# Polysketch attention and an MLP on one core: key-value matrices and all rows of x through DRAM, weight 1 in one piece, a new hand-written order

## The chip, the core and the metric

The kernel runs on one core of a Trainium2 chip. A core has five engines that run at the same time and wait for each other by semaphores: TensorE (PE, matrix products), VectorE (DVE), ScalarE (ACT), GpSimd (POOL) and SyncE (SP, here only an issuer of transfers). Transfers between DRAM and the core's SBUF are issued by SP or ACT and carried out by 16 DMA engines. The metric is the device time of one execution in microseconds (us); less is better.

## The reference

Two blocks follow each other. The first is attention with a sketched polynomial kernel, with 4 batches, 4 heads, 1088 positions and 32 dimensions per head; the second is a layer norm and a two-layer MLP with a residual, on rows of 128 (the four heads side by side).

```python
def phi(x):                                   # r = 8 sketches each
    a = np.einsum('rd,bhsd->bhsr', S1, x)
    b = np.einsum('rd,bhsd->bhsr', S2, x)
    return np.einsum('bhsi,bhsj->bhsij', a, b).reshape(*x.shape[:-1], r * r)
q_p, k_p = (phi(q), phi(k))
kv = np.einsum('bhsf,bhsd->bhfd', k_p, v)     # 64 x 32 for each head
z = np.sum(k_p, axis=2)
num = np.einsum('bhsf,bhfd->bhsd', q_p, kv)
den = np.einsum('bhsf,bhf->bhs', q_p, z)[..., None] + 1e-06
x = (num / den)                               # -> (4, 1088, 128)
...
mu = np.mean(x, axis=-1, keepdims=True)
var = np.mean((x - mu) ** 2, axis=-1, keepdims=True)
xn = (x - mu) / np.sqrt(var + 1e-06) * g_ln
ch = np.maximum(xn @ w_ch1, 0.0) @ w_ch2      # 128 -> 512 -> 128
return (x + ch).astype(np.float32)
```

S1, S2, the two weights and g_ln come as 64-bit floating point where numpy made them so (S and the weights); the kernel has to decode their words itself. All products are in 32-bit floating point.

## The kernel before

Everything is one flat list of named operations, `PROGRAM`: each name calls a small function that issues a few instructions on one or more engines. An engine executes its own instructions strictly in the order of this list, and waits where an operand is not there yet. So the list sets, for each engine and for each issuer of transfers (SP, ACT), what stands in front of what. A letter after a name says which engine does it: S is SP, A is ACT, V is DVE, G is POOL. No planner works at run time.

**Opening.** `ld_w`, `ld_s`, `ld_g`, `ld`, `ld_v`, `ld_vr` load weights, S, g_ln, k and q, and v. `c_...` fill constants; `c_act` is ACT's first activation, which brings a table load with it. `fill n w` and `bump n` are matmuls on ones that nobody reads. The 64-bit words of S (0), weight 1 and weight 2 are decoded by `w_ex`, `w_bits`, `w_exf`, `w_mant`, `w_low`, `w_e2`, `w_e3`, `w_add`/`w_addlow` and `w_mul` on DVE, ACT and POOL; weight 1 in two halves of 256 columns, each with its own load. `s_heads`, `sk`, `sk_b`, `sk_8`, `sk_q` and `sk_2` set up the sketches. `c_cg` and `fold` (with `fold_cp`) put the mean and g_ln of the layer norm into weight 1.

**Attention, per batch b.** `turn_g`/`turn_r` transpose k on DVE; `k_feat` multiplies it with the sketches on PE, `k_tok` transposes the result back, `k_prod` forms the 64 products per position, `k_sum`, `k_zs`, `k_sc`, `k_sccp` work on z, and `k_val` sums products times v into the PSUM bank KV. `k_vcp` (ACT) copies this out four times over, `k_spr` (PE, two 128x128 transposes) turns it, `k_rcp` (ACT) copies the result to `kvr`. For q: `turn_h`/`turn_r`, `q_feat`, `q_tok`, `q_ac`, `q_den`, `q_rec`, `q_a2`, `q_prod` on PE, DVE and POOL give the 64 products per position, already divided by the denominator; `q_turn` transposes them on DVE. `num` then multiplies them with `kvr`: 32 products of 32x32 tiles, each of two matmul instructions, into four PSUM banks, and `num_cp`/`num_r` copy them to `xT`, which holds x transposed. The first half of batch 0 goes another way (`q_dir`, `q_ac0`, `q_b0`, `q_prod0`, `q_flip`, `f_spr`, `num0`), so that the MLP can start early.

**MLP, per chunk c.** Ten chunks: 0 to 7 are half a batch (4 tiles of 128 positions), 8 and 9 collect the left-over positions (1 tile). `hid` multiplies `xT` with one of four column blocks of weight 1 (PE), `relu` copies it out, `sec` (4 products of 128x128 per tile, PE) multiplies with weight 2, and `fin` (DVE), or `fin_a` and `fin_g` (ACT, POOL), scale by 1/std and add x. `store` and `store_r` write the result. For the residual and the statistics x is needed with positions on partitions. For chunks 1 to 7 it goes through DRAM: `row_turn` (DVE), `row_wr` (one write), `row_rd` (four reads per chunk). For chunks 0, 8 and 9 PE transposes it: `row_pe`, `row_cp`. `st_bn`, `st_ag` (DVE) and `st_pow` (POOL) form 1/std.

## Time and profile before

| what | value |
|---|---|
| median of 3 runs | 103.91 us (103.06 to 104.55) |
| profiled execution | 102.81 us, span 100.9 us, granted PE clock 0.998 |
| PE busy | 95.3 us, 94% of the span |
| DVE busy | 74.0 us, 73% |
| POOL busy | 58.4 us, 58% |
| ACT busy | 41.3 us, 41% |
| chain that ended last | PE 78%, DMA 5%, POOL 5%, DVE 2%, ACT 2% |
| moved by DMA | 13.85 MB in 12367 packets |

How to read the rows of the prediction: in a timeline or chain the first number is the start in us from the span's start, the second the duration in us; then engine, line of the kernel, operation, and `out<-in`; `x4` is a count of instructions put together. PEld is PE's weight load, which overlaps its matmuls. SPq and ACTq are transfers issued by SP or ACT. A bracket tells how long the engine sat idle before, and what ended that. In the 40 slices of the span each digit is a busy share in tenths.

### The profile page before, as it was taken

The page shows a single profiled execution, that of the slowest core. Times are in us where ns is not written, and L with a number is a line of the kernel's source. Part 1 is how long each engine was busy: PE and PEld are TensorE (multiplying, and loading weights), DVE is VectorE, ACT ScalarE, POOL GpSimd, SP SyncE. Part 2 cuts the span into 40 slices and gives each one's busy share as a digit, 9 for nine tenths or more (in the row PEclk, how much of TensorE's full clock was granted, in tenths as well). Part 3 has the DMA queues.
Part 4 walks back from the last instruction along what each step waited for, and adds up shares of the span by engine and source line. Part 5 has one row for each costly group of instructions (what it writes and reads, how often), then busy time and mean ns, then how long its engine had stood idle before and what let it go on. Part 6 is the DMA issues. An engine that isn't in the chain of part 4 may idle for free.

```text
span 100.9 us, 3433 instructions
## 1 busy us (share of the span) xinstructions
PE 95.3 (94%) x1355; PEld 68.7 (68%) x1355; DVE 74.0 (73%) x239; ACT 41.3 (41%) x119; POOL 58.4 (58%) x83
## 2 busy tenths in 40 slices
PE   5988999999999999999999999999999999999960
PEld 5765668656656779656588669854469758959950
DVE  2878989789999599699089549999559079661630
...
PEclk9999999999999999999999999999999999999999
...
GB/s 76 272 293 389 353 370 275 272 218 88 3 6 301 212 164 3 6 130 0 6 107 106 47 59 0 109 153 187 55 107 204 143 122 148 1 115 132 77 119 64
DMA packets 12367, 13.85 MB, mean 137 GB/s; under 512 B 2880, under 2 KB 8768, under 8 KB 12352
## 3 DMA queue, kind: packets, MB, share of 16 engines
...
## 4 chain that ended last, share of the span: by engine, by line
PE 78%; DMA 5%; POOL 5%; DVE 2%; ACT 2%; SPq 2%; issue 1%; ACTq 0%; POOLq 0%
PE bankO L859 8%; PE bankM L859 8%; DMA w_raw<-in_moe_w_ch_dram 5%; PE bankN L843 5%; PE bankK L560 5%; PE bankC L843 4%; PE bankK L843 4%; PE bankK L859 4%; PE bankB L843 3%; PE bankA L843 3%; PE bankD L843 3%; PE bankM L250 3%; PE bankA L859 3%; PE bankN L859 3%; POOL ob L888 2%; PE bankA L735 2%
## 5 line engine op out<-in xcount | busy, mean ns | idle before, releaser
L82 POOL TENSOR_TENSOR kp<-kf 128x1024 f32<-128x1024 f32 (+4 forms) x9 | 15.9, 1779 | 0.1
L827 POOL TENSOR_SCALAR va<-mv 128x4 f32<-128x4 f32 (+1 forms) x10 | 2.3, 228 | 18.2 <-DVE mv L822 17.7
L82 POOL TENSOR_TENSOR qp<-a,fq 128x1280 f32<-128x1280 f32 (+1 forms) x5 | 11.1, 2219 | 0.2
L859 PEld LDWEIGHTS bankO<-w,hT 128*128 128x128 f32 x80 | 9.7, 192 | 1.9 <-issue 1.9
L829 POOL TENSOR_TENSOR rstd<-va,mhalf 128x4 f32<-128x4 f32 (+1 forms) x10 | 10.3, 1034 | 0.8
L859 PE MATMUL bankO<-w,hT 128*128 128x128 f32 x80 | 10.4, 277 | 0.0
L859 PEld LDWEIGHTS bankM<-w,hT 128*128 128x128 f32 x72 | 9.0, 192 | 1.9 <-issue 1.9
L677 DVE STREAM_TRANSPOSE qpT<-qp 128x1280 f32<-128x1280 f32 (+1 forms) x7 | 9.6, 1365 | 0.0
L250 PE MATMUL bankM<-ones 128*128 128x256 f32 (+1 forms) x28 | 8.3, 440 | 1.2 <-DVE top L180 1.2
L859 PE MATMUL bankM<-w,hT 128*128 128x128 f32 x72 | 9.3, 275 | 0.0
L816 DVE BATCH_NORM_STATS2 st<-x 128x6 f32<-128x128 f32 x32 | 6.7, 272 | 2.5 <-issue 2.5
L250 PEld LDWEIGHTS bankM<-ones 128*128 128x128 f32 x28 | 5.7, 241 | 2.5 <-DVE top L180 1.2
L851 ACT ACTIVATE hT<-bankC 128x512 f32<-128x512 f32 (+1 forms) x6 | 3.3, 551 | 8.3 <-PE bankB L859 4.7
L843 PE MATMUL bankC<-xT,w 128*128 128x512 f32 x12 | 6.1, 592 | 0.0
L843 PE MATMUL bankN<-xT,w 128*128 128x512 f32 (+1 forms) x14 | 6.1, 516 | 0.0
L851 ACT ACTIVATE hT<-bankN 128x256 f32<-128x256 f32 (+1 forms) x6 | 3.0, 498 | 7.2 <-PE bankN L843 7.2
L82 POOL TENSOR_TENSOR a<-fq,rden 128x160 f32<-128x160 f32 (+1 forms) x6 | 2.8, 463 | 5.2 <-DVE rden L659 4.8
L560 PEld LDWEIGHTS bankK<-kp,vn 128*32 128x32 f32 x288 | 4.2, 110 | 2.3 <-issue 1.1
L851 ACT ACTIVATE hT<-bankK 128x512 f32<-128x512 f32 (+1 forms) x6 | 3.1, 522 | 6.2 <-PE bankK L843 5.3
L457 DVE STREAM_TRANSPOSE qT<-qn 128x512 f32<-128x512 f32 x8 | 5.5, 687 | 0.0
L843 PE MATMUL bankK<-xT,w 128*128 128x512 f32 (+1 forms) x12 | 5.4, 530 | 0.0
L735 PE MATMUL bankD<-qpT,kvr 32*32 32x288 f32 (+1 forms) x64 | 5.2, 386 | 0.0
...
## 6 DMA issues: line engine op xcount, KB each, us to landing
...
xd<-xh SPq DMA_DIRECT2D x5, 256.0 KB, 2.6
x<-xd SPq DMA_DIRECT2D x20, 64.0 KB, 2.0
out_dram<-ob SPq DMA_DIRECT2D x19, 64.0 KB, 1.7
out_dram<-ob ACTq DMA_DIRECT2D x13, 64.0 KB, 1.9
w_raw<-in_moe_w_ch_dram SPq DMA_DIRECT2D x2, 256.0 KB, 4.0
```

Source lines behind the costliest of these rows:

```text
L82: by[eng].tensor_tensor(out=o, in0=a, in1=b, op=ALU.mult)
L250: pe.matmul(M[0][:, 0:w], ones[:, 0:P], ones[:, 0:w], start=True, stop=True)
L457: dve.transpose(_ap(dst[b % 2], 0, P, P * 4 * half, [[32, 4], [P, 4], [1, 32]]), src[b][:, 512 * half : 512 * half + 512],)
L560: pe.matmul(KV[D * h : D * h + D, 0:F], vn[b][:, TW * h + D * u : TW * h + D * (u + 1)], kp[:, H * F * u + F * h : H * F * u + F * (h + 1) ...
L677: dve.transpose(_ap(qpT, 0, P, 32 * u0, [[32, u1 - u0], [TW, 8], [1, 32]]), qp[:, H * F * u0 : H * F * u1])
L735: pe.matmul(X[r][D * h : D * h + D, o : o + w], kvr[b % 2][rows, DM * f + D * h : DM * f + D * h + D], qpT[rows, c : c + w], start=(f == 0 ...
L816: dve.bn_stats(out=sts[slot(c)][:, 6 * t : 6 * t + 6], in_=row_ap(c, t))
L827: pool.tensor_scalar(out=vas[slot(c)][:, 0:n], in0=_ap(mvs[slot(c)], 0, P, 1, [[2, n]]), scalar1=1e-6, scalar2=None, op0=ALU.add)
L829: pool.tensor_tensor(out=rstds[slot(c)][:, 0:n], in0=vas[slot(c)][:, 0:n], in1=mhalf[:, 0:n], op=ALU.pow)
L843: pe.matmul(banks[z][:, 0:n], w1[:, P * j : P * (j + 1)], cols(c)[:, a : a + n], start=True, stop=True)
L851: act.activation(o, i, AF.Relu)
L859: pe.matmul(banks[z][:, DM * t : DM * (t + 1)], h[:, 512 * j + P * t : 512 * j + P * (t + 1)], w2[:, DM * j : DM * (j + 1)], start=(j == 0 ...
```

## The change

1. Weight 1 is loaded by one transfer (`ld_w S 1 0 4`, the first on SP) and decoded in one piece of 512 columns; `fold` and `fold_cp` also run in one piece. `ld_s A 1` now stands behind `c_act`.
2. `k_vcp`, `k_spr` and `k_rcp` are gone. Instead DVE transposes the KV bank in 32x32 blocks (`kv_turn`), one transfer writes it to DRAM (`kv_wr`), four transfers read it back into `kvr`, one for each group of 32 partitions (`kv_rd`).
3. `num` reads `kvr` in the new layout, and its inner loops change places: r (row group of the array) is now innermost, h (column group) outside it.
4. Chunks 0, 8 and 9 go through DRAM as well: `row_pe` and `row_cp` are not called any more.
5. Nearly all transfers are issued by SP: ACT keeps `ld_s A 1` and four stores at the end.
6. The order of the list is new throughout; three `fill 1 256` are added, `sk_0` is dropped, and some operations change engine (`sk_2` and `k_sccp 0` to DVE, `w_mant` of weight 2 to ACT, its `w_add` to DVE, and single `relu`, `num_cp`, `num_r`, `k_prod`, `q_ac`, `q_a2`, `q_prod` between engines).

```diff
-    kvc = const([P, 2 * P], F32, "kvc")
+    kvt = const([P, F], F32, "kvt", 2)
+    kvx = [dram.tile([P, F], F32, name=f"xdk{i}") for i in range(B)]
...
-    def k_vcp(eng, b):
-        copy(eng, _ap(kvc, 0, P, 0, [[P, 2], [32, 4], [1, 32]]),
-             _ap(KV, 0, P, 0, [[32, 2], [0, 4], [1, 32]]))
...
-    def k_spr(b):
-        for i in range(2):
-            pe.transpose(KV[:, 256 + P * i : 256 + P * (i + 1)], kvc[:, P * i : P * (i + 1)], ident)
...
-    def k_rcp(eng, b):
-        copy(eng, kvr[b % 2], KV[:, 256:512])
+    def kv_turn(b):
+        dve.transpose(kvt[b % 2], KV[:, 0:F])
...
+    def kv_wr(eng, b):
+        by[eng].dma_start(out=bass.AP(kvx[b].tensor, kvx[b].offset, [[F, P], [1, F]]), in_=kvt[b % 2])
...
+    def kv_rd(eng, b, r):
+        by[eng].dma_start(
+            out=_ap(kvr[b % 2], 32 * r, 32, 0, [[F, H], [1, F]]),
+            in_=bass.AP(kvx[b].tensor, kvx[b].offset, [[F, 32], [32 * F, H], [1, F]]),
+        )
...
     def num(b, u0, u1):
         w = 32 * (u1 - u0)
         for f in range(2):
-            for r in range(4):
-                for h in range(H):
+            for h in range(H):
+                for r in range(4):
...
-                        kvr[b % 2][rows, DM * f + D * h : DM * f + D * h + D],
+                        kvr[b % 2][rows, F * h + D * f : F * h + D * f + D],
...
-    through_dram = set((1, 2, 3, 4, 5, 6, 7, ))
+    through_dram = set((0, 1, 2, 3, 4, 5, 6, 7, 8, 9))
```

The new list, cut to the parts that the prediction follows (the opening up to `num 1`, and the stretch from `num 2` to `num 3`):

```diff
+    c_ones; ld_w S 1 0 4; c_small; c_kvb; ld_s S 0; fill 1 128; c_act; ld_s A 1; c_iota; c_vpad 3;
+    ld S k 0 16 34; c_pads 0; fill 4 256; c_rest; ld S k 0 0 16; c_vpad 2; c_ac 1; ld S q 0 16 34;
+    c_pads 1; c_ac 0; c_ident; ld_h S q 0 0; ld S v 0 0 32; w_bits V 0 0 32; c_m8; w_mant A 0 0 32;
+    w_ex V 0 0 32; w_addlow V 0 0 32; ld S k 1 0 34; w_exf A 0 0 32; w_ex V 1 0 512; w_e2 A 0 0 32;
+    w_bits V 1 0 512; ld_g S; w_exf A 1 0 512; c_m2; ld_v S 1 1; fill 1 256; w_e3 V 0 0 32; c_m32;
+    s_heads G; w_mant A 1 0 512; turn_g k 0 2 4; ld_vr S 1 1; fill 1 128; fill 1 128; sk;
+    w_low A 1 0 512; fill 1 256; ld_vr S 0 0; turn_g k 0 0 2; sk_8 A; fill 1 256; sk_q;
+    w_e2 A 1 0 512; turn_r k 0; sk_b; sk_qq 0; w_add G 1 0 512; k_feat 0 0 9; sk_2 V; ld_vr S 0 1;
+    fill 1 256; k_tok 0 0 0 9; bump 24; k_tok 0 1 0 9; ld_vr S 1 0; turn_r q 0; w_e3 V 1 0 512;
+    k_prod G 0 6 9; k_sum 0; fill 1 128; k_zs 0; fill 1 256; sk_d; turn_h q 0 0; k_sc 0;
+    ld S q 1 0 34; v_flip 1 B; v_flip 3 A; k_sccp V 0; v_flip 0 C; turn_h q 0 1; fill 1 128;
+    v_flip 2 O; k_prod G 0 0 3; v_cp A 0 C; q_dir 0 4 N; k_sccp F 0; v_cp A 3 A; v_cp A 1 B;
+    ld_w S 2 0 4; turn_g k 1 0 4; ld S k 2 0 34; q_feat 0 4 9; q_cp A 0 4 N 16 24; v_cp A 2 O;
+    k_prod G 0 5 6; fill 1 256; q_ac0 0 4 N 0; fill 1 256; c_vpad 0; q_tok 0 1 4 9; k_prod G 0 3 5;
+    q_den 0 0 4; fill 1 256; q_tok 0 0 4 9; turn_r k 1; bump 12; q_rec 0 0 4; q_tok 0 2 4 9;
+    c_vpad 1; w_mul G 1 0 512; k_feat 1 0 9; q_b0 0 4 N 0; q_tok 0 3 4 9; k_val 0; q_prod0 2 4 N 0;
+    q_ac G 0 4 9; q_prod0 0 2 N 0; q_flip 2 4 0 M; f_vcp A; q_den 0 4 9; q_flip 0 2 1 C;
+    q_flcp A 2 4 0 M; q_rec 0 4 9; q_flip 2 4 1 D; c_cg V; q_flcp A 0 2 1 C; q_flip 0 2 0 N;
+    turn_h q 1 1; q_a2 G 0 4 9; q_flcp A 2 4 1 D; f_spr O; fold C 0 512; q_flcp A 0 2 0 N;
+    q_prod G 0 4 9; kv_turn 0; f_rcp A O; k_tok 1 0 0 9; w_low A 2 0 512; kv_wr S 0; k_tok 1 1 0 9;
+    num0 0 2 N; ld_v S 1 2; turn_h q 1 0; k_sum 1; ld_v S 1 3; num0_cp A 0 2 N; num0 2 4 M;
+    fold_cp A C 0 512; k_zs 1; ld_v S 1 0; turn_r q 1; w_ex V 2 0 512; k_sc 1; kv_rd S 0 0;
+    num0_cp A 2 4 M; hid O 0 3 0 2; sk_qq 2; k_prod G 1 0 5; k_sccp V 1; kv_rd S 0 3;
+    turn_g k 2 0 4; q_feat 1 0 9; kv_rd S 0 2; ld_vr S 2 1; hid M 0 3 2 4; q_tok 1 2 0 9;
+    kv_rd S 0 1; hid N 0 1 2 4; turn_r k 2; relu A M 0 3 2 4; ld S k 3 0 34; q_tok 1 3 0 9;
+    hid K 0 0 0 2; relu A N 0 1 2 4; q_tok 1 1 0 9; k_prod G 1 5 9; hid C 0 2 2 4;
+    relu A O 0 3 0 2; ld_vr S 2 0; w_exf A 2 0 512; q_tok 1 0 0 9; hid N 0 2 0 2; q_turn 4 9;
+    hid D 0 0 2 4; relu A K 0 0 0 2; relu A N 0 2 0 2; k_feat 2 0 9; ld S q 2 0 34;
+    relu A C 0 2 2 4; relu A D 0 0 2 4; q_ac G 1 0 4; w_e2 A 2 0 512; k_val 1; k_tok 2 0 0 9;
+    q_ac G 1 4 9; k_tok 2 1 0 9; w_bits V 2 0 512; num 0 4 9; row_turn 0; w_mant A 2 0 512;
+    row_wr S 0; k_sum 2; num_cp A 0 1 4 8; num_cp V 0 2 4 8; ld_v S 2 0; num_cp A 0 3 4 8;
+    hid M 0 1 0 2; num_cp A 0 0 4 8; kv_turn 1; w_add V 2 0 512; ld_v S 2 1; hid N 1 3 0 4;
+    kv_wr S 1; w_e3 V 2 0 512; ld_v S 2 2; hid C 1 0 0 4; q_den 1 4 9; w_mul G 2 0 512; ld_v S 2 3;
+    q_rec 1 4 9; q_den 1 0 4; row_rd S 0 2; hid O 1 2 0 4; k_zs 2; relu A C 1 0 0 4; row_turn 1;
+    relu A N 1 3 0 4; q_rec 1 0 4; hid K 1 1 0 4; turn_g k 3 0 4; num_r A 0; q_a2 G 1 0 4;
+    relu A O 1 2 0 4; q_prod G 1 0 4; sec M 0 2; relu A K 1 1 0 4; turn_r k 3; kv_rd S 1 0;
+    turn_h q 2 1; k_sc 2; kv_rd S 1 2; k_feat 3 0 9; turn_h q 2 0; kv_rd S 1 3; sec O 1 3;
+    k_sccp V 2; q_a2 G 1 4 9; kv_rd S 1 1; relu V M 0 1 0 2; row_rd S 0 0; turn_r q 2;
+    q_prod G 1 4 9; k_tok 3 1 0 9; sec O 1 0; row_rd S 0 3; k_tok 3 0 0 9; row_rd S 0 1;
+    q_turn 0 4; q_feat 2 0 9; ld_v S 3 1; row_wr S 1; k_sum 3; ld S q 3 0 34; sec M 0 3;
+    k_prod G 2 5 9; q_tok 2 3 0 9; q_tok 2 1 0 9; sec M 0 1; k_zs 3; q_tok 2 2 0 9; q_tok 2 0 0 9;
+    sec M 0 0; q_turn 4 9; q_ac G 2 4 9; k_prod G 2 0 5; sec O 1 1; k_sc 3; num 1 0 9; k_sccp V 3;
...
+    q_ac V 3 0 4; q_ac G 3 4 9; q_den 3 0 4; q_rec 3 0 4; num 2 0 9; kv_turn 3; st_bn 1; kv_wr S 3;
+    store S 0 2 0 4; q_den 3 4 9; store S 0 3 0 4; q_rec 3 4 9; sec N 3 3; num_cp A 2 0 0 4;
+    num_cp V 2 3 4 8; row_rd S 2 1; num_cp A 2 0 4 8; q_a2 G 3 4 9; num_cp V 2 2 4 8; num_r A 2;
+    num_cp A 2 1 0 4; st_ag 1; num_cp A 2 1 4 8; store S 0 1 0 4; num_cp V 2 2 0 4; sec M 2 0;
+    st_pow 1; row_rd S 3 3; num_cp V 2 3 0 4; hid C 8 2 0 1; relu V N 8 0 0 1; hid A 8 1 0 1;
+    hid K 4 2 0 4; row_turn 4; q_prod G 3 4 9; relu A A 8 1 0 1; relu A C 8 2 0 1; row_wr S 4;
+    sec N 3 0; kv_rd S 3 2; st_bn 3; kv_rd S 3 0; hid A 4 3 0 4; row_turn 5; hid C 8 3 0 1;
+    st_ag 3; hid B 5 3 0 4; row_wr S 5; q_turn 4 9; relu A C 8 3 0 1; fin_a O 1; kv_rd S 3 1;
+    hid C 4 0 0 4; row_rd S 4 1; row_rd S 8 2; relu A K 4 2 0 4; st_pow 3; st_bn 2; hid O 5 0 0 4;
+    row_rd S 4 2; relu A A 4 3 0 4; row_rd S 4 0; relu A C 4 0 0 4; st_ag 2; hid A 4 1 0 4;
+    kv_rd S 3 3; fin_g G 1; sec K 8 0; relu A A 4 1 0 4; q_a2 G 3 0 4; fin_a N 3; row_rd S 5 3;
+    hid C 5 2 0 4; st_pow 2; q_prod V 3 0 4; row_rd S 4 3; row_rd S 5 1; sec K 4 2; row_rd S 5 2;
+    fin_g G 3; q_turn 0 4; fin_a M 2; row_rd S 8 3; hid A 5 1 0 4; store S 1 2 0 4;
+    relu V C 5 2 0 4; sec K 4 1; fin_g G 2; relu A A 5 1 0 4; relu V B 5 3 0 4; relu A O 5 0 0 4;
+    sec N 4 0; st_bn 4; store S 2 3 0 4; num 3 0 9; store S 1 3 0 4; st_bn 8; row_rd S 5 0;
...
```

More of the change, by code (lines that the diff above doesn't have):

```diff
@@ L947 @@
-    st_bn 0; ld S q 3 0 34; q_a2 G 1 4 9; sec M 0 1; q_rec 1 0 4; k_zs 2; turn_g k 3 0 4;
-    q_a2 G 1 0 4; hid K 1 3 0 4; q_prod G 1 0 4; relu V O 1 1 0 4; sec M 0 0; relu A K 1 3 0 4;
-    turn_h q 2 1; relu A D 1 0 0 4; k_sc 2; k_feat 3 0 9; relu A N 0 3 2 4; q_prod G 1 4 9;
-    k_sccp V 2; relu A C 1 2 0 4; k_val 1; k_tok 3 0 0 9; k_tok 3 1 0 9; row_rd S 1 3; q_turn 0 4;
-    ld_v S 2 0; k_sum 3; q_feat 2 0 9; ld_v S 3 2; k_vcp A 1; sk_qq 3; row_rd S 1 1; st_ag 0;
-    k_spr 1; q_tok 2 1 0 9; sec M 0 2; ld_v S 2 2; k_rcp A 1; q_tok 2 2 0 9; ld_v S 3 3;
@@ new lines @@
+    row_rd S 3 1; q_turn 0 4; row_rd S 8 1; sec M 2 1; row_rd S 3 0; q_tok 3 1 0 9; k_val 3;
+    q_ac V 3 0 4; q_ac G 3 4 9; q_den 3 0 4; q_rec 3 0 4; num 2 0 9; kv_turn 3; st_bn 1; kv_wr S 3;
[3 more added lines that the diff above has]
+    st_pow 1; row_rd S 3 3; num_cp V 2 3 0 4; hid C 8 2 0 1; relu V N 8 0 0 1; hid A 8 1 0 1;
```

118 lines of the change are left out of this document (34 added, 84 removed).

## The prediction

> **What bounds the kernel now.** I read the page first, then the chain that ended last in order of time, then the timeline of the first 21 us, then the waits of SP.
>
> ```profile
> span 100.9 us, 3433 instructions
> PE 95.3 (94%) x1355; PEld 68.7 (68%) x1355; DVE 74.0 (73%) x239; ACT 41.3 (41%) x119; POOL 58.4 (58%) x83
> PE   5988999999999999999999999999999999999960
> PEclk9999999999999999999999999999999999999999
> ```
>
> TensorE is busy in every slice from the third on, at full granted clock. No other engine comes near that over the whole span, and the 41 and 58 of ACT and POOL leave room everywhere. But the busy share of a pipelined PE says little alone, and the first slices hold warming matmuls (`fill`, `bump`) that nobody needs. The chain shows from where PE does nothing but needed work:
>
> ```profile
> 11.62 0.51 PE bankM L250 x2
> ...
> 20.79 0.37 PE bankK L575 x2
> 21.16 0.36 PE bankA L629
> 21.61 0.14 PE bankA L629
> 21.85 0.63 PE bankK L843 x2
> ...
> 23.78 0.44 PE bankO L787 x4
> ...
> 40.63 0.38 PE bankA L735 x4
> ...
> 42.16 1.09 PE bankO L859 x8
> ...
> 44.11 0.11 PE bankD L787
> 44.22 0.86 PE bankK L843 x2
> ...
> 96.47 0.91 PE bankA L859 x8
> 97.40 0.35 DVE ob L872
> ```
>
> The first `hid` is at 21.85. From there PE runs needed work without a hole to 97.40: 75.55 us. Behind that stands a tail of 3.5 us (last `fin`, last store, its landing). Before 21.85 the kernel is a chain of latencies over DMA, DVE and ACT. So two numbers set the end: **when the first `hid` can start, and how much PE work is left then**. The time of an edit on any other engine counts only if it moves the first, or opens a hole in the second.
>
> **PE work that goes.** Each `k_spr` (two transposes, L575) takes 0.37. Four are removed, one of them before 21.85, so 3 x 0.37 = 1.11 goes from the full stretch. `row_pe` of chunk 0 (L787, four transposes) is 0.44, of chunks 8 and 9 it is 0.11 each: 0.66. One item comes in: before, `q_feat` of batch 1 (L629, from 21.16 to 21.85: 0.70) is done ahead of the first `hid`; in the new order it stands behind it. +0.70.
>
> **The reordered `num`.** It is the same 64 matmul instructions of 32x32, and from 40.63 to 42.16 they take 1.53. The PE timeline shows how:
>
> ```profile
> 40.56 0.45 PE L735 MATMUL bankA<-qpT,kvr 32*32 32x288 f32 x4
> ...
> 40.82 0.42 PE L735 MATMUL bankA<-qpT,kvr 32*32 32x288 f32 x4
> ...
> 41.06 0.65 PE L735 MATMUL bankA<-qpT,kvr 32*32 32x288 f32 x5
> 41.31 0.47 PE L735 MATMUL bankB<-qpT,kvr 32*32 32x288 f32 x4
> ```
>
> Groups of 16 start 0.25 apart (40.56, 40.82, 41.06), but within the third group bank B follows bank A by 0.25, where in the groups ahead the banks follow each other closely: the second half `f` cannot load its weights into a row group that is still working, because four successive matmuls share it. With `r` innermost, successive matmuls go to different row groups. `q_feat` does so already: 32 instructions in 0.70, so twice that would be 1.40, a gain of 0.13; the whole hole is 0.22. Below nothing I keep 0.1, as `q_feat` adds nothing up in PSUM and so bounds it only loosely. I take the hole, nearly: 0.2 for each of three full `num` and 0.1 for the short one, 0.7; the range keeps -0.1 to 0.9. The Trainium skill, "TensorE: Matmul & The Clock Gate", Part 3, The mechanism, says that a weight load overlaps a running matmul only when its row group differs; by that rule the whole 0.22 goes each time, and the sum would be 0.1 to 0.2 lower.
>
> Work left at the first `hid` is then 75.55 - 1.11 - 0.66 - 0.70 + 0.70 = **73.8**. The three added `fill 1 256` (0.51 each by the row at 11.62) all stand ahead of the first `hid`, where PE waits for DVE; if that cover were gone they would cost 1.5.
>
> **When the first `hid` starts.** The rows of the opening:
>
> ```profile
> 1.17 0.60 ACTq L104 DMA_DIRECT2D s_raw<-in_S_dram  x1
> ...
> 1.80 1.28 ACT L184 ACT_TABLE_LOAD   x1 [1.80 <-issue]
> ...
> 3.72 0.17 DVE L277 TENSOR_SCALAR ex<-s_raw 16x32 uint32<-16x32 uint32 x1 [0.38 <-DMA s_raw<-in_S_dram]
> ...
> 5.82 0.51 ACT L311 ACTIVATE ex<-exf,top 128x256 uint32<-128x256 f32 x1
> ...
> 6.70 0.23 DVE L452 STREAM_TRANSPOSE kT<-kn 128x64 f32<-128x64 f32 x1
> ...
> 7.08 0.40 PE L506 MATMUL bankA<-kT,sk 64*32 64x288 f32 x1 [0.28 <-DVE kT L452]
> ...
> 7.40 0.40 PE L506 MATMUL bankB<-kT,sk 64*32 64x288 f32 x1
> ...
> 8.71 0.47 DVE L516 STREAM_TRANSPOSE kf<-bankA 128x288 f32<-128x288 f32 x1
> ...
> 17.25 0.67 DVE L82 TENSOR_TENSOR qp<-bankO,a 128x512 f32<-128x512 f32 x1
> ...
> 20.36 1.23 DVE L434 STREAM_TRANSPOSE kT<-kn 128x1024 f32<-128x1024 f32 x1
> ...
> 21.10 0.72 ACT L288 ACTIVATE exf<-ex,m 128x512 f32<-128x512 uint32 x1
> ...
> 39.75 1.45 DVE L82 TENSOR_TENSOR kp<-kf 128x1280 f32<-128x1280 f32 x1
> ```
>
> Step 1, S. Before, ACT issues its half of S at 1.17, ahead of its table load. In the new order `c_act` comes first, so the issue waits for the 1.28 of the table: about 2.0 to 2.2 instead of 1.17, and S is decoded from 4.7 instead of 3.72. +1.0.
> Step 2, to `k_feat` of batch 0. Before, it starts 3.36 after S. Ahead of `sk_8`, ACT ran three half-width passes of 0.51 on weight 1; now it runs three full-width ones of 0.72. +0.6. So `k_feat` starts at 4.7 + 3.36 + 0.6 = 8.7 instead of 7.08.
> Step 3, given back. `k_tok` began at 8.71, 0.9 after the last `k_feat` matmul (7.40 + 0.40), because DVE was decoding the second half of weight 1. That work now lies earlier, so `k_tok` follows at once, at 8.7 + 0.7 = 9.4. Only 0.7 of the 1.6 is left.
> Step 4, DVE from `k_tok` to `turn_g k 2`: 8.71 to 20.36, 11.65. The new list is 0.9 longer (all of `w_e3`, `c_cg`, `kv_turn`, two `k_sccp`, less `sk_0`). With the same pauses, about 1.0 in all, `turn_g k 2` starts at 22.0; with none, at 21.0. I take 21.5.
> Step 5. Before, the last `q_prod0` ended at 17.92, 2.4 ahead of `turn_g k 2`; the flips, ACT's copies and `num0` then took 3.9 to the first `hid`. In the new order more of DVE's other work lies behind `q_prod0`, which so stands about 3.5 ahead of `turn_g k 2`, at 18.0, and ACT has one copy less (`k_vcp`): first `hid` at **21.5**, between 21.0 and 22.0.
>
> **Weight 1 and the loads.** One load of 512 KB heads SP's queue.
>
> ```profile
> w_raw<-in_moe_w_ch_dram SPq DMA_DIRECT2D x1, 512.0 KB, 7.2
> ...
> DMA to landing us min/median/max: 2.7/5.3/7.2
> ...
> xd<-xh SPq DMA_DIRECT2D x5, 256.0 KB, 2.6
> x<-xd SPq DMA_DIRECT2D x20, 64.0 KB, 2.0
> ...
> L808 SPq DMA_DIRECT2D x<-xd x20: 303/423/511, 32.0 to 84.2; - x20
> ...
> SPq L808 <- DMA xd<-xh: 16.5, 5, 9.4
> ```
>
> The first half of weight 1, with nothing ahead of it, landed in 2.7; weight 2, as big as the new load but behind a full queue, in 7.2. Between these ends I take 4.0, as nothing is ahead: it lands at 4.7, before DVE's `w_ex V 1 0 512` wants it at about 5.5. k of batch 0 comes less than 1 later and is wanted later too; q and v0 have the second load of k no longer ahead of them. Cost in the sum: nothing, covered by step 2.
>
> **DRAM trips and SP.** I count 137 transfers on SP instead of 81, and 5 on ACT instead of 27. At 0.42 each SP issues for 58 of 99 us. A trip of a key-value matrix is `kv_turn` (DVE; about 0.2, by the 128x64 transpose at 6.70), a write (2.6), four reads (2.0 and 3 x 0.42): some 6.5 from `k_val`. The new order leaves 9 (batch 0) to 16 us of PE work between `k_val` and its `num`, so it is hidden; were it not, it would cost up to 6.5 less what is left. Rows 0, 8 and 9 make the trip with 10 us and more before their `fin`. On DVE, three `row_turn` and four `kv_turn` replace the half-width decoding and `st_bn 0`, which moves back: from `turn_g k 2` to the second `q_turn` of batch 1 the list is as long as before (20.36 to 39.75, 19.4). So `num 1` may start at 21.5 + 19.4 = 40.9; PE's own work up to there is 8 half and 4 full `hid` (0.43 and 0.86, row at 44.22), 7 `sec` (0.89 to 0.91, row at 96.47) and some 6 of attention, 19.0: it arrives at 40.5. No hole worth a term. The Trainium skill, "DMA: Bandwidth & Descriptors", Rules for kernel authors, speaks against all this: transfers under 64 KB are mostly overhead, and `kv_rd` moves 32 KB. By that rule, as an estimate, 35 added transfers of small size pay their fixed cost each; it enters the sum only where PE waits for one, which is the rival C below.
>
> **The sum.** PE ends at 21.5 + 73.8 = 95.3 instead of 97.4. The tail stays 3.5 (the last `fin`, then two stores). The span goes from 100.9 to 98.8. The profiled execution took 102.81 against a median of 103.91, so I carry the difference, -2.1, to the median: **101.8**.
>
> **Rivals.**
> A, the forecast; its own range is 101.1 to 103.1 (start 21.0 to 22.0, `num` -0.1 to 0.9 where 0.7 is taken).
> B, **the load decides**: weight 1 lands after 7.2, at 7.9. `w_ex` on DVE holds up S behind it, 2.4 later than wanted at 5.5, and the gain is gone: 104.2. For it: 512 KB did take 7.2. Against: that one was not first in line.
> C, **SP is late for `num 3`** (slower). One in-order queue now carries everything. Behind `kv_wr 3` stand two stores, `row_rd 2 1`, a store, `row_rd 3 3`; for the last, `st_bn 3` holds DVE, then `row_turn 5`, `row_wr 5` and five more issues until `kv_rd 3 3`. From `num 2` on: 1.4 + five issues 2.1 + landing 2.0 + DVE 1.3 + six issues 2.5 + landing 2.0 = 11.3; PE has 15.2 of work there (7 `sec`, 8 full `hid`, 3 of 0.22, and `num`). So it decides once SP stands still for more than 3.9 at that place. Before, SP's longest stand for a DRAM trip was 9.4; put there it costs 9.4 - 3.9 = 5.5: 107.3. For it: ACT no longer offers a second queue. Against: in before, such stands were mostly waits with nothing due.
> D, **the joints go too**: PE's rows add up to 74.0 for the 75.55 after the first `hid`, so 1.5 lies in small joints, and DVE had pauses of 1.0 before it. Without DVE's pauses (start 21.0) and with 1.0 less of joints: 95.3 - 0.5 - 1.0 = 93.8, 100.3.
>
> **Chances.** A 0.52, D 0.18, C 0.25, B 0.05. Two per cent, about what a measurement of this kernel can tell from no change, lies at 101.83, in the middle of A, so A gives half to each side: faster 0.26 + 0.18 = 0.44, same 0.26 + 0.05 = 0.31, slower 0.25. The range goes from 100.0 (D with a little more) to 107.3 (C).
>
> **What would show it.** Right: L575 and L787 gone, a full `num` at 1.3 to 1.35, first `hid` near 21.5, `num 1` near 41, no PE idle row longer than 0.3 after that, last `fin` near 95.3. Step 1 is wrong if S is decoded before 4.3. Wrong altogether: PE waiting before L735 on a DMA into `kvr` or on DVE (C), or DVE's `w_ex` waiting for `w_raw` (B).

## The result, and the profile after

The changed kernel takes **106.15 us** (median of 6 runs, 105.97 to 108.33); on the same chip the kernel before took 104.08 (102.96 to 104.55). The ratio is 1.029, with a 95% interval of 1.025 to 1.033: slower, where 101.8 and faster was forecast. All ratios compare only executions within 1.5 per cent of the fastest of their kernel, so a ratio need not be the quotient of two medians. The profiled execution took 106.07 us. Its page, in the lines that answer to those of before:

```profile
span 104.3 us, 3428 instructions
PE 96.3 (92%) x1345; PEld 68.6 (66%) x1345; DVE 75.1 (72%) x230; ACT 38.3 (37%) x111; POOL 59.3 (57%) x82
PE   5959999994999999999999999999999989998960
PEclk9999999999999999999999999999999999999999
```

The clock is full, as before. New is the 4 in the tenth slice (23.5 to 26 us): TensorE stands still, after it has begun with needed work. The waits of PE, and the two stretches from the first `hid` to the end (first before, then after; the columns are the stretch, its length, busy time of PE, PEld, DVE, ACT, POOL, the granted clock, the DMA share and GB/s):

```profile
PE bankA L629 <- DVE skq L554: 1.3, 1, 1.3
...
PE bankC L843 <- DVE ob L872: 0.5, 1, 0.5
PE bankD L859 <- DVE ob L872: 0.4, 1, 0.4
```

```profile
21.78:97.36 75.58, 75.46 (x991) 55.14 (x980) 56.08 (x177) 28.33 (x81) 43.20 (x47) 1.00 0.34 98
```

```profile
22.81:100.71 77.90, 75.72 (x1002) 54.57 (x1001) 59.64 (x176) 27.09 (x82) 44.14 (x45) 1.00 0.45 128
```

PE's work ends 3.35 later than before: 1.03 because the first `hid` starts later, 2.32 because the stretch behind it is longer. From the starts of all PE rows in these stretches, each row's time counted to the next start, it divides so (us):

| | before | after | difference |
|---|---|---|---|
| `k_spr` and `row_pe` | 1.58 | 0 | -1.58 |
| `num` | 5.70 | 5.81 | +0.11 |
| `q_feat` (batch 1 now behind the first `hid`) | 1.41 | 2.11 | +0.70 |
| `hid` and `sec` | 60.96 | 61.93 | +0.97 |
| idle | 0.11 | 2.18 | +2.07 |
| `k_feat`, `k_sum`, `k_sc`, `k_val` | 5.82 | 5.87 | +0.05 |

The idle time is one wait of `q_feat 1` (1.3) and two at the end (0.9). The chain of work that ended last names the holder of the first:

```profile
20.07 1.10 PE bankC L360 x2
21.16 0.58 PE bankN L715 x4
21.75 0.33 PE bankK L532 x18
22.07 0.02 issue
22.10 0.19 DVE zT L540
22.29 0.15 DVE qT L452
22.44 2.20 DVE ex L277
24.64 0.11 DVE skq L554
24.75 0.04 issue
24.80 0.42 PE bankA L629
```

2.2 us stand there under one VectorE instruction, `w_ex V 2 0 512`, which the prediction did not name. In VectorE's and GpSimd's timelines of the changed kernel, and in VectorE's of before:

```profile
22.36 2.28 DVE L277 TENSOR_SCALAR ex<-w_raw 128x512 uint32<-128x512 uint32 x1
```

```profile
21.98 4.46 POOL L82 TENSOR_TENSOR kp<-kf 128x1280 f32<-128x1280 f32 x2
```

```profile
16.97 0.36 DVE L277 TENSOR_SCALAR ex<-w_raw 128x512 uint32<-128x512 uint32 x1
```

The same shape took 0.36 before, in a gap between two GpSimd instructions. In the new order it meets GpSimd's two products `k_prod G 1`, and ends at 24.64, soon after the first of them must (an estimate: half of 4.46 behind 21.98 is 24.2).

### The profile page after: what moved, and what is told of

It reads as the page before. It is cut to its first block, busy times and chain, and to the rows that moved or that the text cites. A ratio compares the mean times of both kernels' runs of the same rounds, so it can differ in the third digit from the quotient of the medians.

```text
span 104.3 us, 3428 instructions
## 1 busy us (share of the span) xinstructions
PE 96.3 (92%) x1345; PEld 68.6 (66%) x1345; DVE 75.1 (72%) x230; ACT 38.3 (37%) x111; POOL 59.3 (57%) x82
## 4 chain that ended last, share of the span: by engine, by line
PE 73%; DMA 9%; DVE 8%; SPq 2%; issue 2%; ACT 2%; POOL 0%; DVEq 0%
PE bankM L859 8%; PE bankN L859 6%; PE bankC L843 5%; PE bankO L859 5%; PE bankA L843 4%; PE bankK L561 4%; PE bankM L250 4%; DMA s_raw<-in_S_dram 3%; PE bankK L859 3%; PE bankB L843 3%; PE bankK L843 3%; PE bankA L735 3%; DVE ex L277 3%; PE bankA L507 2%; PE bankM L843 2%
## 5 line engine op out<-in xcount | busy, mean ns | idle before, releaser
L82 POOL TENSOR_TENSOR kp<-kf 128x1280 f32<-128x1280 f32 (+4 forms) x9 | 16.3, 1820 | 0.7 <-DVE kf L517 0.6
L859 PEld LDWEIGHTS bankN<-w,hT 128*128 128x128 f32 x56 | 6.9, 191 | 1.9 <-issue 1.9
L859 PE MATMUL bankN<-w,hT 128*128 128x128 f32 x56 | 7.7, 280 | 0.0
L859 PE MATMUL bankO<-w,hT 128*128 128x128 f32 x48 | 6.4, 279 | 0.0
L843 PE MATMUL bankC<-xT,w 128*128 128x512 f32 (+1 forms) x12 | 5.8, 566 | 0.5 <-DVE ob L872 0.5
L859 PEld LDWEIGHTS bankO<-w,hT 128*128 128x128 f32 x48 | 5.8, 192 | 0.6 <-issue 0.5
L888 POOL TENSOR_TENSOR ob<-ob,x 128x512 f32<-128x512 f32 x4 | 6.1, 1519 | 0.0
L797 DVE STREAM_TRANSPOSE xh<-xT 128x512 f32<-128x512 f32 x8 | 5.6, 695 | 0.6 <-ACT xT L77 0.6
L735 PE MATMUL bankC<-qpT,kvr 32*32 32x288 f32 (+1 forms) x64 | 5.9, 385 | 0.0
L735 PE MATMUL bankB<-qpT,kvr 32*32 32x288 f32 (+1 forms) x64 | 5.9, 386 | 0.0
```

The source lines that it names most:

```text
L82: by[eng].tensor_tensor(out=o, in0=a, in1=b, op=ALU.mult)
L735: pe.matmul(X[r][D * h : D * h + D, o : o + w], kvr[b % 2][rows, F * h + D * f : F * h + D * f + D], qpT[rows, c : c + w], start=(f == 0), ...
L797: dve.transpose(_ap(xh[slot(c)], 0, P, 0, [[32, n], [32 * n, 4], [1, 32]]), cols(c))
L843: pe.matmul(banks[z][:, 0:n], w1[:, P * j : P * (j + 1)], cols(c)[:, a : a + n], start=True, stop=True)
L859: pe.matmul(banks[z][:, DM * t : DM * (t + 1)], h[:, 512 * j + P * t : 512 * j + P * (t + 1)], w2[:, DM * j : DM * (j + 1)], start=(j == 0 ...
L888: by[eng].tensor_tensor(out=o, in0=o, in1=i, op=ALU.add)
```

## The experiments

The theory T from these rows: VectorE's instruction is held by GpSimd's product, and the late opening and stalls at the end add to it. Rivals: R1, the trips through DRAM and the one queue cost the time; R2, the late sketch matrices do. Ratios are to the kernel before on the same chip, with 95% intervals; medians of different chips are not compared.

**e1: the held instruction, out of the product's way.**

```
-  turn_r q 1; w_ex V 2 0 512; k_sc 1;
+  q_prod0 0 2 N 0; w_ex V 2 0 512; q_flip 2 4 0 M;
```

> The changed kernel with one instruction of VectorE moved: the exponents of weight 2 are taken right after the last q_prod0 (about 18.3 us), where GpSimd has nothing to do until 18.96, instead of at 22.36, where GpSimd multiplies kp. T (VectorE's instruction is held by GpSimd's two-input product): it takes 0.36 to 0.41 us in place of 2.28; k_sccp 1 stands at about 23.0 in place of 24.57, q_feat 1 at about 23.4 in place of 24.80, and the time falls by 1.3 to 1.9 to some 104.3 to 104.9 us. R1 (the trips through DRAM and the one queue cost the time): the instruction's place matters for nothing, within 0.3 of the changed kernel's 106.15. R2 (the late sketch matrices cost it): as R1. If the 2.28 is a mark of the instruction's data and not of its neighbour, it stays at 2.28 at the new place.

105.11 us, ratio 1.017 (1.010 to 1.024). The instruction took

```profile
18.03 0.41 DVE L277 TENSOR_SCALAR ex<-w_raw 128x512 uint32<-128x512 uint32 x1
```

`q_feat 1` started at 23.20 without a wait, and PE ended at 99.33 instead of 100.71. T's mechanism holds, and the two intervals (this one and 1.025 to 1.033) do not overlap. In size it is 1.2 per cent by the ratios, some 1.2 us, just under T's 1.3.

**e2 and its repetition e2b: the same instruction put beside a product in the kernel before.**

```
-  q_rec 0 4 9; fill 1 128; f_vcp A; w_ex V 2 0 512;
+  ld_v S 1 3; w_ex V 2 0 512; k_sccp V 1;
```

> The kernel before with the same one instruction moved the other way: from 16.97, where GpSimd has nothing to do, to just ahead of k_sccp 1 at about 20.3, while GpSimd multiplies kp (20.07 to 22.0). T: it takes 1.7 to 2.0 us in place of 0.36, q_feat 1 goes from 21.09 to 22.3 to 22.8, and the time rises by 1.0 to 1.7 from 104.1 to 105.1 to 105.8. R1 and R2: 0.4 us on VectorE at most, hidden, within 0.4 of the kernel before.

> The kernel before with weight 2's exponents moved beside GpSimd's product of kp, once more: the first time the instruction took 1.95 us (22.68 to 24.63, the product 22.28 to 24.22) but the run's clock was 0.96 and its time said nothing. T: at the full clock it takes 1.7 to 2.0 us, q_feat 1 goes from 21.09 to 22.3 to 22.8, and the time rises by 1.0 to 1.7 over the kernel before. Rival (the wait is hidden in the whole): the instruction is as long, the time within 0.5 of before.

VectorE's and GpSimd's timelines of e2b:

```profile
20.73 1.92 DVE L277 TENSOR_SCALAR ex<-w_raw 128x512 uint32<-128x512 uint32 x1
```

```profile
20.28 1.94 POOL L82 TENSOR_TENSOR kp<-kf 128x1024 f32<-128x1024 f32 x1
```

It is 1.95 us long in e2 and 1.92 in e2b, and ends 0.4 after the product both times: the neighbour makes the length, not the data. On the time little can be said. One execution of each run kept the full clock; they took 104.42 and 104.59, which is 1.15 and 1.02 over the median of those executions of before that count beside them (103.27 and 103.57), as T said. The other six, both profiled ones among them, ran at a mean clock of 0.961 to 0.984 and took 106.5 to 109.8; in the two traces the clock falls at the hole (last section). So no interval can be given.

**e3: `num` in its old order.**

```
-            for h in range(H):
-                for r in range(4):
+            for r in range(4):
+                for h in range(H):
```

> The changed kernel with the two inner loops of num in the order of before (row group outside, head inside), the new layout of the key-value matrices kept. The prediction gave the new order 0.2 us for each full num, 0.7 in all. T, from the traces (a full num took 1.53, 1.54 and 1.52 us after, 1.53 before): the order is worth nothing, within 0.2 of the changed kernel. Rival: the new order did bring 0.2 each and the layout or the shared PSUM banks ate it; then a full num takes 1.7 us here and the time rises by 0.7.

106.34 us, ratio 1.031 (1.022 to 1.039): no difference. PE's timeline of the changed kernel at the start of the second half of `num 1`, with a matmul of the first half and a weight load of the second on the same tile:

```profile
44.58 0.40 PE L735 MATMUL bankA<-qpT,kvr 32*32 32x288 f32 x1
...
44.82 0.40 PE L735 MATMUL bankA<-qpT,kvr 32*32 32x288 f32 x1
45.02 0.42 PE L735 MATMUL bankB<-qpT,kvr 32*32 32x288 f32 x1
```

```profile
44.59 0.40 PE L735 MATMUL bankB<-qpT,kvr 32*32 32x288 f32 x1
...
45.01 0.10 PEld L735 LDWEIGHTS bankB<-qpT,kvr 32*32 32x32 f32 x1
```

and of e3:

```profile
44.48 0.65 PE L735 MATMUL bankA<-qpT,kvr 32*32 32x288 f32 x5
44.73 0.47 PE L735 MATMUL bankB<-qpT,kvr 32*32 32x288 f32 x4
```

The hole is there in both orders: 0.20 from 44.82 to 45.02, and in e3 0.20 as well by the single records (44.48 to 44.68; the row merges five matmuls, so that bank B seems to follow by 0.25). The weight loads suggest what it is. Both halves use the same 16 tiles of the array, and the second weight load of the second half starts at 45.01, when the first half's last matmul on that tile has just ended (44.59 and 0.40: 44.99); in e3's records it is 44.67 after 44.65. At that moment all four row groups still work on the first half, so no order of r and h inside a half avoids it. This reading fits both orders; no run tests it by itself.

**e4 and e5: the sketch matrices earlier.** e4 issues ScalarE's half ahead of `c_act`; e5 in addition issues SyncE's half ahead of weight 1.

```
-  c_ones; ld_w S 1 0 4; ... ld_s S 0; fill 1 128; c_act; ld_s A 1;
+  c_ones; ld_s S 0; ld_w S 1 0 4; ... fill 1 128; ld_s A 1; c_act;
```

> The changed kernel with ScalarE's load of the second sketch matrix ahead of c_act, as in the kernel before, so that it isn't issued behind the table load. S is decoded at about 3.7 in place of 4.88. R2 (the late opening costs the time): k_feat 0 and the first kp about 1.1 earlier, and the time falls by 2 to the kernel before's 104.1. T: the opening moves up by 0.8 to 1.1, the held instruction on VectorE with it (its GpSimd neighbour moves up as well and still takes it along), and the time falls by 0.6 to 1.1 to 105.0 to 105.5. R1: within 0.3 of the changed kernel.

> The changed kernel with both loads of the sketch matrices issued first of all: SyncE's ahead of weight 1, ScalarE's ahead of the table load. The run that moved ScalarE's alone got S at 4.6 instead of 4.9, right after weight 1, so S waits for weight 1's 512 KB and not for its own issue. If that is so, S is decoded at 3.0 to 3.8 here and the decoding of S, k_feat 0 and the first kp all come 0.6 to 1.2 earlier. R2 (the late opening costs the time): the time falls by as much or more, to 105.0 or below. T (VectorE's instruction held by GpSimd, and joints behind it): the opening's gain reaches the first hid, and the time falls by 0.4 to 1.0 at most, since the held instruction stays at 2.2 to 2.3 us. If the opening is bounded by the arrival of k and q instead, nothing: within 0.2.

106.35 (1.031, 1.023 to 1.039) and 106.22 (1.031, 1.026 to 1.037): nothing. In e4 S is decoded at 4.54, in e5 at 2.41, against 4.88. So S had waited for weight 1's 512 KB and not for the table load. The changed kernel's own trace shows the same of the table load: ScalarE issues its half of S at 1.18, as before (1.17), while the table load still runs.

```profile
0.72 1.28 ACT L184 ACT_TABLE_LOAD   x1 [0.72 <-PEq L1022]
1.18 0.59 ACTq L104 DMA_DIRECT2D s_raw<-in_S_dram  x1
```

But the first `kp` moved only from 10.81 to 10.59, because VectorE's next two instructions need weight 1 (e5, VectorE's and ScalarE's timelines):

```profile
4.85 0.43 DVE L277 TENSOR_SCALAR ex<-w_raw 128x512 uint32<-128x512 uint32 x1 [1.58 <-DMA w_raw<-in_moe_w_ch_dram]
```

```profile
5.31 0.72 ACT L288 ACTIVATE exf<-ex,m 128x512 f32<-128x512 uint32 x1 [1.25 <-DVE ex L277]
5.94 0.70 ACT L296 ACTIVATE mant<-bits,one 128x512 f32<-128x512 uint32 x1
6.55 0.65 ACT L304 ACTIVATE low<-w_raw 128x512 f32<-128x512 uint32 x1
7.57 0.44 ACT L410 ACTIVATE sk<-bankK,m 128x16 f32<-128x16 f32 x2 [0.37 <-PE bankK L374]
```

R2 falls in the form "S is late". What is late is all that stands behind weight 1's decoding: S's last step on VectorE first of all, and `sk_8`, which waits 0.37 more for its product behind ScalarE's three passes.

**e9: weight 1's decoding behind the sketch.** To e5 comes:

```
-  w_ex V 0 ...; w_ex V 1; w_exf A 0; w_bits V 1; w_exf A 1; ... w_mant A 1; ... w_low A 1; ... turn_g k 0 0 2; sk_8 A; sk_q; w_e2 A 1;
+  turn_g k 0 2 4; ... w_ex V 1; w_bits V 1; turn_g k 0 0 2; sk_8 A; sk_q; w_mant A 1; w_low A 1; w_exf A 1; w_e2 A 1;
```

> The changed kernel with S loaded first and, this time, weight 1's decoding put behind S's: on VectorE its two first steps stand between the two halves of k (they stood ahead of S's last step and of k), on ScalarE its three first steps stand behind sk_8 and sk_q. Early S alone brought the first kp only from 10.81 to 10.59, since VectorE then stood 1.58 us waiting for weight 1 and ScalarE had 2.1 us of weight 1 ahead of sk_8. W (weight 1 in one piece ahead of the sketch is what makes the opening late): the first kp comes at 8.7 to 9.5, k_val 0 at 15.8 to 16.5 in place of 17.70, first hid and q_feat 1 1.2 to 1.9 earlier, and the time falls by 1.2 to 1.9 to 104.3 to 105.0. Rival (the opening is bounded by the arrival of k and q): first kp not below 10.3, time within 0.4 of 106.15. Rival (GpSimd's chain of products from the first kp to k_val decides, not its start): the first kp earlier, k_val 0 within 0.5 of 17.7.

107.98, ratio 1.045 (1.032 to 1.057): worse. The first `kp` came at 9.62, as W said, but `k_val 0` at 17.91. The gain was lost at one place (VectorE's timeline):

```profile
10.46 1.22 DVE L318 SCALAR_TENSOR_TENSOR bits<-w_raw,ex 128x512 uint32<-128x512 uint32 x1 [0.89 <-ACT ex L311]
11.60 0.18 DVE L540 TENSOR_TENSOR zT<-bankK,m 128x32 f32<-128x32 f32 x1
```

`w_e3 V 1` now waits for ScalarE's later steps, with `zT` and the turns of q queued behind it, and stands beside a GpSimd product (1.22 for 0.65 in e5). That explains why nothing was gained, not why e9 is slower than the changed kernel: its profiled execution (108.09) lost clock, at a mean of 0.984, but two others at 0.998 and 0.999 took as long (108.13 and 107.88). That part stays open.

**e6, e10: the end.** e6 issues three stores ahead of `row_wr 7` and puts `st_bn 9` behind chunk 7's `fin`. e10 gives six stores of chunks 1 to 3 to ScalarE, behind its last copy of `num 3`.

```
e6   + store S 2 1; store S 1 0; store S 1 1;   row_turn 7; st_bn 5; row_wr S 7;
e6     fin B 7 1; + st_bn 9; st_ag 9; st_pow 6; + st_pow 9;
e10    num_cp A 3 1 4 8; + store A 2 1; store A 2 2; store A 2 0; store A 3 1; store A 1 0; store A 1 1;
```

> The changed kernel with its end relieved: the three stores of chunks 1 and 2 that free the output buffers late are issued ahead of row_wr 7 and row_wr 9, and st_bn 9, st_ag 9 and st_pow 9 stand behind the sums of chunk 7. T (the end's stalls of TensorE, 0.48 for bank C behind fin C 5 1 and 0.4 for bank D behind fin D 7 0, each with what follows it, are part of the loss): TensorE's waits for these two go, the time falls by 0.4 to 0.9 to 105.3 to 105.8. R1 (the one queue is the cause in general): the stores only change places with the rows of 7 and 9, which now come later: within 0.2, or slower by up to 0.5.

> The changed kernel with six stores of chunks 1, 2 and 3 (those that SyncE issues between 79 and 85 us) issued by ScalarE behind its last copy of num 3, where it has nothing to do from 80.2 to 83.6. Putting stores ahead of the writes of rows on the same queue only moved the end's stalls from bank C to bank D (0.94 in one place for 0.48 and 0.39 in two). Q (at the end one queue at 0.43 to 0.46 us an issue is the bound): the reads of rows 6, 7 and 9 are issued 2 to 2.7 us earlier, both waits of TensorE go, and the time falls by 0.6 to 1.0 to 105.2 to 105.6. Rival (DRAM's answer, not the issue, sets the reads): waits stay, within 0.2 of the changed kernel.

What PE waits for there is, in the changed kernel, VectorE's `fin C 5 1`, which waits for a store, and `fin D 7 0` behind `st_bn 9`, which waits for a read. SyncE issues both kinds one behind the other:

```profile
79.01 2.33 SPq L893 DMA_DIRECT2D out_dram<-ob  x5
```

```profile
85.49 0.35 DVE L872 SCALAR_TENSOR_TENSOR ob<-bankC,rstd,x 128x128 f32<-128x128 f32 x1 [2.60 <-DMA out_dram<-ob]
...
95.37 0.29 DVE L816 BATCH_NORM_STATS2 st<-xr 128x6 f32<-128x128 f32 x1 [1.38 <-DMA xr<-xd]
```

e6: 106.13, 1.032 (1.027 to 1.037), nothing; the two waits of PE became one of 0.94 for bank D, as the rows of chunk 6 came later. e10: 105.22, 1.020 (1.010 to 1.031), 0.9 per cent less, but the interval overlaps that of the changed kernel, so by the times alone this is not shown. In its trace the wait for bank C went, the one for bank D stayed (0.5), and PE ended 1.01 earlier, 0.38 of it gained in the opening already, which varies by some tenths between executions. So in one queue a store and a read only changed places; with six issues taken out, some 0.6 came back.

**e7, e8: one part alone in the kernel before.** e7 has the key-value matrices through DRAM (`kv_turn`, `kv_wr` at the places of `k_vcp`, the `kv_rd` at those of `k_spr`). e8 issues 20 of ScalarE's row transfers and stores on SyncE.

```
e7   - k_vcp A b; ... k_spr b; ... k_rcp A b;
e7   + kv_turn b; kv_wr S b; ... kv_rd S b 0; kv_rd S b 1; kv_rd S b 2; kv_rd S b 3;
e8   - row_wr A ..; row_rd A ..; store A ..;   + row_wr S ..; row_rd S ..; store S ..;
```

> The kernel before with one part of the change alone: the key-value matrices turned on VectorE and spread through DRAM (one write, four reads on SyncE) in place of the two transposes on TensorE and the two copies on ScalarE; num reads them in the new layout, its loops stay. The prediction's term: three batches at 0.37 us of TensorE, 1.11 less, if no num waits for its reads. T: 0.5 to 1.1 faster than before, 103.0 to 103.6, with a wait of num 1 (k_val 1 ends at 35.6 there, num 1 starts at 40.6, and the trip takes about 5) that may eat up to 0.8 of it. R1 (the trips through DRAM cost the time): slower than before by 1 or more, num waiting for kvr in all three batches.

> The kernel before with another part alone: the writes and reads of rows and the stores that ScalarE issues go to SyncE (20 of them), at their old places in the order; the last three stores stay with ScalarE as after the change. R1 (one queue for nearly all transfers costs the time): slower than before by 1.5 to 3 us. T: ScalarE has 20 issues of 0.4 us less, SyncE has slack at nearly all of them; within 0.5 of the kernel before, with more waits of st_bn for x in the second half.

e7: 103.69, 1.002 (0.995 to 1.009). e8: 102.73, 0.999 (0.993 to 1.004). R1 falls as far as the kernel before goes: neither part makes it slower. e7 gained nothing either, so T's 0.5 fell too: `num 1` takes 2.22 instead of 1.53, since its reads for banks C and D are late (chain of e7), and that eats most of the 0.83 that the three `k_spr` took:

```profile
40.61 0.07 PE bankB L735 x4
40.68 0.52 PE bankC L735 x8
```

**e11 to e14: together.** e11 is e1, e9 and e10. e12 is e1 and e10. e13 adds e9's opening with `w_e3 V 1` moved to ahead of `q_ac0`, where VectorE is idle. e14 adds TensorE's order: `k_val 0` ahead of `k_feat 1`, `f_spr`, `f_rcp` and `fold` ahead of the `q_flip`s.

```
e13  - turn_r q 0; w_e3 V 1 0 512;          + w_e3 V 1 0 512; q_ac0 0 4 N 0;
e14  - k_feat 1 0 9; ... k_val 0; ... f_vcp A;   + k_val 0; f_vcp A; k_feat 1 0 9;
e14  + c_cg V; w_e3 V 1;   f_spr O; f_rcp A O; fold C 0 512; q_flip 2 4 0 M;   q_flip 0 2 1 O (for C)
e14  + q_flcp A 0 2 0 N; fold_cp A C 0 512;    w_low A 2; sk_qq 2;
```

> The changed kernel with the three edits together: weight 2's exponents in GpSimd's gap, S and its decoding ahead of weight 1's, six stores with ScalarE. If the three causes are separate: 1.0 (measured) + 1.2 to 1.9 + 0.6 to 1.0 off 106.15, that is 102.2 to 103.3, faster than the kernel before (104.1). If one stands behind another (GpSimd's products now decide the time of q_feat 1 by themselves): 103.5 to 104.5, as before.

> The changed kernel with the two edits that each gained 0.9 to 1.0: weight 2's exponents in GpSimd's gap, six stores with ScalarE. If they are separate losses at two ends of TensorE's row, they add up: 106.15 - 1.0 - 0.9 = 104.2, the kernel before's time. If the end's stall only moves when all comes earlier: 104.8 to 105.1.

> e12 with S and its decoding ahead of weight 1's, as in e9, and with w_e3 V 1 moved on VectorE from ahead of zT to ahead of q_ac0, where VectorE has nothing to do. W (the late start of the products makes the opening late): first kp at 9.6, k_val 0 at 16.0 to 16.7 in place of 17.70, and 1.0 to 1.3 less than e12, 102.9 to 103.2. Rival (TensorE's order around k_val 0 decides): k_val 0 not below 17.2, within 0.4 of e12.

> e13 with TensorE's order changed: k_val 0 ahead of k_feat 1 (which waits for turn_r k 1 on VectorE), f_spr, f_rcp and the fold ahead of the q_flips, c_cg earlier, the fold's copy ahead of num0's, weight 2's low words behind them. M (half of the opening's loss is this order: k_val 0 starts 1.45 us after the last kp, and 1.1 us of fold stand ahead of num0): num0 1.0 to 1.5 earlier than in e13, first hid 0.6 to 1.2 earlier, the time 0.5 to 1.0 less than e13. Rival (the q side on VectorE decides: q_prod0 and the flips): num0 within 0.4 of e13, the time too.

e11: 105.10, 1.016 (0.997 to 1.035): too wide to tell, with e9's fault in it. e12: 104.33, 1.015 (1.010 to 1.020). e13: 103.74, 1.008 (1.004 to 1.012). e14: 104.09, 1.012 (1.008 to 1.016). The traces' milestones (us; starts, and PE's end):

| | S | first `kp` | `k_val 0` | `num0` | first `hid` | `q_feat 1` | `num 3` | PE ends |
|---|---|---|---|---|---|---|---|---|
| before | 3.72 | 9.63 | 15.68 | 19.14 | 21.78 | 21.09 | 72.12 | 97.36 |
| after | 4.88 | 10.81 | 17.70 | 21.09 | 22.81 | 24.80 | 77.24 | 100.71 |
| e1 | 4.68 | 10.60 | 17.49 | 20.88 | 22.60 | 23.20 | 75.70 | 99.33 |
| e10 | 4.50 | 10.43 | 17.31 | 20.70 | 22.42 | 24.42 | 76.86 | 99.70 |
| e12 | 4.72 | 10.68 | 17.57 | 20.96 | 22.68 | 23.28 | 75.72 | 98.33 |
| e13 | 2.28 | 9.69 | 16.48 | 19.87 | 21.59 | 22.20 | 74.76 | 97.36 |
| e14 | 2.29 | 9.57 | 15.59 | 20.06 | 21.77 | 22.38 | 74.95 | 98.16 |

In the traces the edits add up: 1.38 (e1) and 1.01 (e10) make 2.39, and e12 ends 2.38 earlier. That it fits so closely is luck, since the openings differ: counted from the first `hid`, 1.17 and 0.62 stand against 2.25. e13 takes 0.97 more, and PE ends where it ended before. By the ratios the steps are smaller: e1 and e10 gave back 1.2 and 0.9 of the 2.9 per cent, e12 only 1.4, and e13 0.7 more. The profiled executions of e1, e12 and e13 are each the fastest of their run (e13's took 102.77, its median is 103.74), so the traces show these edits at their best; by the ratio e13 is still 0.8 per cent slower than before, and where that lies is not shown. M fell: `k_val 0` came 0.9 earlier and `num0` 0.2 later, because `num0` then waited 0.63 for ScalarE's copy of the flips.

**e15 to e17: is there more in it?** e15 is e13 with the last reads of chunks 6 and 9 ahead of four stores; e16 adds `k_val 0` ahead of `k_feat 1`; e17 is e7 with `k_val 1` and its trip earlier.

```
e15  + row_rd S 7 3; row_rd S 6 0; row_rd S 6 1; row_rd S 6 2; row_rd S 9 0; row_rd S 9 2; store S 4 3;
e16  + k_val 0; f_vcp A; k_feat 1 0 9;
e17  + k_val 1; sec M 0 0; ... kv_turn 1; turn_h q 2 1; ... kv_wr S 1; k_tok 3 0; ... ld_v S 2 0; kv_rd S 1 0..3;
```

> e13 with the last reads of rows (chunk 6 and chunk 9) ahead of four stores on SyncE. In e13 st_bn 6 waited 1.19 us and st_bn 9 1.34 us for their reads, and TensorE 0.28 us for bank D with 0.44 us lost in the sum ahead of it. Q: both waits shrink by 1 us, the end comes 0.4 to 0.7 earlier, 103.0 to 103.3 (on the scale on which the kernel before has 104.1: 0.990 to 0.995 of it or equal). Rival (the reads wait for DRAM): as e13, 103.7.

> e15 with k_val 0 ahead of k_feat 1 on TensorE, nothing else of e14's order. If TensorE has work without a gap from k_val 0 on, k_val 0 comes 0.9 earlier and first hid 0.2 to 0.5 earlier, the time 0.2 to 0.5 less than e15. Rival: the flips wait for q_prod0 on VectorE, first hid stays, the time too.

> The kernel before with the key-value matrices through DRAM as in e7, and k_val 1, kv_turn 1, kv_wr 1 and the reads of batch 1 placed some 2 us earlier, so that num 1 has its reads. If the saving on TensorE is real: num 1 takes 1.5 us and not 2.2, and three batches at 0.28 us (the traces' difference between after and before for k_spr, not the prediction's 0.37) give 0.8 less than before. Rival (what is taken from TensorE there is spent at other joints): within 0.3 of before.

e15: 103.25, ratio 0.995 (0.990 to 0.999). e16: **102.93, ratio 0.992 (0.987 to 0.996)**: the mended kernel is somewhat faster than before, by less than one per cent. How much of that is these two edits stays open: e13 ran on another chip, where its ratio was 1.008, and yet from the first `hid` PE's stretch is 75.77 long in both traces, e13's and e15's. So the ratio can shift by a per cent between chips. PE ends at 97.66 in e15's trace and 98.13 in e16's, no earlier than in e13. In e16 the first `kp` happened to come 0.57 later than in e15; counted from it, `k_val 0` came 1.1 and the first `hid` 0.5 earlier, as expected, but the intervals of the two overlap. In e15 `st_bn 6` and `st_bn 9` no longer wait, as Q said, but VectorE then waits at `fin D 7 0`:

```profile
92.52 0.35 DVE L872 SCALAR_TENSOR_TENSOR ob<-bankD,rstd,x 128x128 f32<-128x128 f32 x1 [2.57 <-DMA out_dram<-ob]
```

a store that the reads went past. In e17 the move changes part of what is computed (which part was not found), so its time, ratio 1.005, is not read, and whether the saving on TensorE would show with punctual reads is left open.

## Why the prediction was wrong, point by point

PE's work ended at 100.71 against 95.3 forecast. The traces divide the 5.4: 3.35 is what e1, e10 and e13 give back (1.38 for the held instruction, 1.0 at the end, 0.97 in the opening); 0.1 is the first `hid` of e13 (21.59) against 21.5; the last 2.0 is work left at the first `hid`, 75.77 in e13 and not 73.8. Of that, 0.9 is `num`, 0.64 `hid` with `sec`, 0.2 `k_spr` with `row_pe`, and the rest idle time and small changes.

**Step 1** had the size (4.88 for 4.7) by luck, since its reason was wrong: ScalarE's issue did not wait for the table load (1.18), and S waited behind weight 1's bytes (e4, e5). **Step 2** (`k_feat` at 8.7; it was 9.08) priced the full-width passes of ScalarE, and missed that VectorE and ScalarE stand in order behind weight 1 whenever S comes. Rival B looked for that wait and let it go because weight 1 lands "before DVE's `w_ex V 1 0 512` wants it": true, since S was as late itself. **Step 3** held: `k_tok` followed `k_feat` by 0.8, at 9.89.

**Step 4** is the step that failed first of all; it holds the largest piece with one cause. It walked VectorE's list at the durations of before and put `turn_g k 2` at 21.5; it came at 24.67. 1.9 of this is `w_ex V 2`, for which the walk took 0.36 without asking what GpSimd does then; 0.5 is `k_tok`, later from the start, and 0.8 longer pauses than the walk took (VectorE stands 0.93 ahead of `q_ac0` and 1.04 ahead of `k_zs 1`). `num 1` came at 44.38 for 40.9. The Trainium skill, "SBUF — State Buffer", SBUF: two separate sides, says that VectorE and GpSimd share one pair of ports under an exclusive lock, held for a whole instruction, against a VectorE instruction in a two-port mode or with two SBUF inputs. The traces agree: 0.36 and 0.41 alone, 2.28, 1.95 and 1.92 beside a product. `w_ex` has one SBUF input, so by that rule it would have to run in a two-port mode, which no trace here shows. It was a rule against this change, and the prediction did not weigh it.

**Step 5**: the last `q_prod0` ended at 18.33 for 18.0, but `num0` came at 21.09: four flips, `f_spr` and 1.10 of `fold` stand on PE behind `k_val 0`, which ends at 18.91. The step subtracted on VectorE's list alone; weight 1 in one piece had put the fold into that row.

**PE work**: `k_spr` is 0.28 each by the starts, not 0.37, so 0.83 for 1.11; `row_pe` 0.75 for 0.66; `q_feat` +0.70 as said. **The reordered `num`**, -0.7 in the sum, was +0.1 (after) to +0.2 (e13): the hole stayed, and e3 shows that the order is worth nothing. The prediction read the 0.25 off a merged row and put it down to four successive matmuls in one row group; with all four groups still at work on the first half, the new order had nothing to gain. And `hid` with `sec` came out 0.64 dearer in e13 (61.60 for 60.96): one `sec` product takes 0.99 beside matmuls on narrower tiles (`num`, `q_feat`, `k_feat`, `k_val`, `k_sum`) and 0.89 elsewhere. Counting instructions by their own rows left out what they cost at a change of neighbours. Rival D's joints were not idle time either: PE was busy 75.46 of the 75.58 of before.

**SP**: the trips are hidden as forecast; PE has no wait on `kvr`, and rival C did not occur at `num 3`. `st_bn 3` did stand for 1.88 (VectorE, at 67.40), inside the slack of 3.9. But the step asked only after the reads of `num`, not after the end, where SP's stores and reads at 0.43 to 0.46 an issue fill the queue: 0.9 of idle PE there, of which 0.5 was left in e10 and 0.3 in e12.

The **tail** was 3.6 for 3.5. The forecast's chance of slower, 0.25, lay on the wrong mechanism.
